# Packed attention with a gated convolution: gvl, the weights' sums, x, the last stores and the issue order changed together

## The chip, the cores and the metric

The kernel runs on one core of a Trainium2 chip. The metric is device time in microseconds, the median of several executions. In the texts PE is TensorE, DVE VectorE, ACT ScalarE, POOL GpSimd and SP SyncE, which issues all DMAs here.

## The reference

For 8 batches, 8 heads, 576 positions and a head size of 64, 32 packing queries p per head first attend to k and v; their 32 results are keys and values for the queries q. The 8 heads are put side by side (512 channels) as x. A causal convolution of 5 taps over x makes a gate, x @ w_val a value, and (gate * value) @ w_out is the output. q, k, v and p are float32, the three weights float64.

```python
p_packed = sm_attn(p, k, v)                  # 32 rows per head
out = sm_attn(q, p_packed, p_packed)         # 576 rows per head
x = out.transpose(0, 2, 1, 3).reshape(B, S, H * D)
gate_pre = sum(conv_w[k] * xp[:, k:k + S, :] for k in range(5))
gate = 1.0 / (1.0 + np.exp(-gate_pre))
val = x @ w_val
return gate * val @ w_out
```

## The kernel before

Each batch b goes through the same stages, written as generators: `load_k`, `load_v`, `load_q`, `load_p` (K, V, Q, P in the order), `keys` (k: p and k transposed on TensorE, kpt, kT), `attn_pack` (a: scores s1, softmax, at, pv, and ppd, the packed values twice side by side), `queries` (q: qpt, qT), `packed_turned` (p: ppT), `attn_out` (s: scores s2 of q with the packed keys, turned by VectorE into t, the maximum taken off by GpSimd, exp), `weighted` (t: t divided by its sum on GpSimd, turned back into a2, and split into a2h and a2l, the upper and lower parts in fp32r), `packed_values` (w: wp, packed values times w_val, split into wph and wpl), `mixed` (x), `gate` (g), `value` (v) and `project` (o). A head group g is 4 heads; an n4 or c of `gate`, `value` and `product` is one of 4 blocks of 128 channels. The trace calls s1 and s2 both s, told apart by what they read: s<-kT and s<-qT. In the same way a1 and a2 are called a there.

`mixed` (line 463) makes x, transposed, in PSUM, two halves of 288 positions per head group. For that the packed values pp, masked so that each head has its own columns, are split into pph and ppl, and six fp32r matmuls on tiles of 64 rows and 128 columns add pph·a2h, ppl·a2h and pph·a2l. ScalarE copies x to xp. `gate` (line 503) makes sig from xp: one step on ScalarE, four on VectorE (sig<-xp,cw,sig), and a tanh on ScalarE. `value` (line 523) multiplies sig by val on VectorE (gv), ScalarE rounds that to gvh, and GpSimd takes the difference, gvl; only the very last gvl is made on VectorE. `project` (line 576) has 36 chunks of 128 rows, 4 after an even batch and 5 after an odd one; each is 12 matmuls of 512 columns (gvh·woh, gvh·wol, gvl·woh for 4 blocks), a copy to osb, of which there are two buffers, and a store. The last batch holds its five chunks open in PSUM, and adds the last block to all of them at the end.

The weights come as 64-bit words. `from_double` (line 240) makes of each quarter a float32 upper part (top) and a lower part, in the words' own place: a scaling on ScalarE, and four steps on VectorE, or three and two more on ScalarE and GpSimd. `value_weights` (W, line 267) adds them on GpSimd to wv; `out_weights` (O, line 289) makes woh and wol.

The order of everything is written out in `ORDER` (line 49): each token lets a generator go one step (or so many), and so fixes the order of the instructions on each engine, SP's DMAs too. At the `|` the staging pool of the weights is closed and gvh and gvl are opened in its place. Every instruction is issued by the helper `InOrder`, so nearly all of them have line 94 in the profile.

Of the kernel before, what the change touches and what calls it, by code (L numbers as in the profile page):

```python
# [54 lines left out]
q1 t0 q1 g0 t0 w1 O0 g0 q1.2 w1 O0 q1.2 s1 O0 k2 q1 O0 s1 q1 K2 k2.2 V2 O0 s1 q1 Q2 k2.2 V2 k2 Q2 s1 K3 a2 P4 O0
s1.2 a2 s1 a2 k2 g0 k2.2 s1 g0 t0 v0 k2 g0 s1 t1 k2 s1 x0 v0 t1 k2 k3 | v0 a2 g0 x0 q2 k3 a2 v0 x0 q2 t1 q2 a2.3
x0 g0 v0 a2 q2 g0 x1 t1 x1 a2 q2 a2 t1 a2 q2.2 g0 a2.2 q2 t1 g0 x1 q2 g0 x1 v0 t1 a2 k3 q2 a2 x1 K3 x1 a2 V3 k3
g0 k3 Q3 v0 q2 P5 t1 k3.2 v0 q2 a2 t1 v0 k3 g0 a2 x1 t1 a2.3 g0 k3 a2.2 k3 g0 k3 a2.2 g0 p2 a3 g0 v0 p2 g0 k3.2
s2 v0 a3 k3 k4 v0 s2 a3 q3 s2 a3 q3 V3 g0 Q3 v0 K4 k4 a3 s2 K4 P6 a3.2 g0 a3 q3 s2 w2 g0 a3 q3 t2 g0 x1 a3 q3
a3.2 w2 v0 t2 a3.2 w2 v0 s2 q3 v0 g1 t2 o0 a3.2 t2 a3 g1 t2 s2 v1 o0 g1 s2 a3 g1 q3 a3.2 s2 x1 q3 o0 a3 Q4 o0 V4  # L60
x1 g1 s2 g1 t2 g1 v1 a3 t2 o0 k4 a3.2 o0 v1 g1 x1 k4 V4 t2 a3 v1 p3 x1 v1 a3 p3 t2 g1 x2 s3 t2 g1 q3 k4 s3 x2
q3.2 k4 o0 g1 q3 Q4 s3 g1 x2 g1 s3 v1.2 g1 q4 s3 k4 v1 q4.2 o0 K5 s3 k4 o0 q4 g1 k4 a4 s3 k4.2 g1 v1 k4 s3 g1 o0
a4 s3 g1.2 v1 a4 g1 s3 g1 v1 x2 o0 q4 g1 x2.2 o0 v1 q4 Q5 q4 x2 v1 q4 g1.2 x2.2 t3 g2 k4 v1 t3 x2 q4 K5 k4 k5 x2
v1 P7 g2 a4 q4 t3 x2 v1 o1 k5 a4 t3 x3 g2 a4.2 x3 t3 a4 o1 k5 t3 a4.2 o1 v2 k5 a4 g2 t3 a4 o1 a4 g2 t3 g2.2 v2
t3 q4 g2 v2 k5 Q5 t3 a4 q4 k5 g2 k5 o1 V5 w3 a4.2 v2 o1 k5 a4 K6 a4 k5 g2 a4.2 w3 o1 g2 k5 w3 a4 x3 g2.3 v2 o1
g2 o1 g2 o1 v2 g2 v2 g2 v2 g2 v2 o1 g2 o1 k5 g2 a4 x3 k5 v2 a4.2 g2 x3.2 v2 g2 V5 k5 a4 x3 a4 p4 v2 a5 K6 k5 p4
v2 g2 a5 x3 g3 a5 g3 o1 v2 g3 v2 g3 a5 v2 o1 v3 o1 a5 g3 a5 o2 a5 g3.2 v3 g3 v3 g3 a5 o2 k6 s4 v3 a5 o2 k6 x3 s4
q5 x3 a5 g3 x3 q5 a5 v3 s4 x3 g3 x4 s4 g3 a5 q5 g3 v3 o2 x4 s4 x4 g3 a5 q5 v3 t4 v3 a5 o2 s4 o2 a5.2 t4 V6 a5.2
q5 s4 a5.2 v3 q5 Q6 g3 a5 t4 g3 q5 t4 a5 s4 k6 q5 a5 w4 g3 k6 t4 g3 q5 k6 s4 g3 v3 a5 k6 w4 g3 x4 V6 o2 v3 g3 s4
# [590 lines left out]
```

## Time and profile before

| what | us |
|---|---|
| median of 3 runs | 331.21 (329.43 to 331.38) |
| profiled execution | 330.79 |
| its span, first to last instruction | 329.0 |
| PE / DVE / ACT / POOL busy in it | 287.6 / 259.0 / 215.3 / 123.2 |

The span is what the profile shows; some 1.8 us lie around it. Busy times overlap, and none of them is the time of the kernel. A group of rows names what an instruction writes and reads as out<-in, by the program's names without their numbers.

### The profile page before, as it was taken

The page shows a single profiled execution, that of the slowest core. Times are in us where ns is not written, and L with a number is a line of the kernel's source. Part 1 is how long each engine was busy: PE and PEld are TensorE (multiplying, and loading weights), DVE is VectorE, ACT ScalarE, POOL GpSimd, SP SyncE. Part 2 cuts the span into 40 slices and gives each one's busy share as a digit, 9 for nine tenths or more (in the row PEclk, how much of TensorE's full clock was granted, in tenths as well). Part 3 has the DMA queues.
Part 4 walks back from the last instruction along what each step waited for, and adds up shares of the span by engine and source line. Part 5 has one row for each costly group of instructions (what it writes and reads, how often), then busy time and mean ns, then how long its engine had stood idle before and what let it go on. Part 6 is the DMA issues. An engine that isn't in the chain of part 4 may idle for free.

```text
span 329.0 us, 7252 instructions
## 1 busy us (share of the span) xinstructions
PE 287.6 (87%) x2932; PEld 220.6 (67%) x2932; DVE 259.0 (79%) x381; ACT 215.3 (65%) x440; POOL 123.2 (37%) x115
## 2 busy tenths in 40 slices
PE   0157987979989999999999898989999999999990
PEld 0134744657758877877877677776868868778870
DVE  0794288689999999997797999998997899776600
ACT  0347788779986779777686867776677755655201
POOL 1334536374153455323245434415431237323200
PEclk9999997699999999999999999999999999999996
DMA  7999989495895765383507491635011011211013
GB/s 197 232 255 263 257 162 239 108 230 108 211 217 135 187 166 136 90 241 92 157 34 173 118 237 37 175 87 126 32 66 34 32 35 38 70 53 64 34 24 135
DMA packets 42474, 43.47 MB, mean 132 GB/s; under 512 B 6085, under 2 KB 36805, under 8 KB 42442
## 3 DMA queue, kind: packets, MB, share of 16 engines
q1 hardware_dynamic: 42442, 43.02, 53.6%
q8 instruction: 23, 0.38, 0.5%
q14 instruction: 9, 0.07, 0.1%
HBM read 33.57 MB, written 9.44 MB: 131 GB/s over the span
## 4 chain that ended last, share of the span: by engine, by line
PE 40%; DVE 31%; ACT 17%; issue 4%; DMA 3%; POOL 3%; SPq 1%; ACTq 0%; POOLq 0%
DVE sig L94 16%; PE o L94 15%; PE val L94 8%; ACT sig L94 4%; DVE a2l L94 3%; PE x L94 3%; PE s L94 3%; PE kpt L94 3%; PE pv L94 2%; DVE sm L94 2%; PE at L94 2%; DVE t L94 2%; DVE nb L94 2%; DMA wv_words<-in_moe_w_val_dram 2%; PE qpt L94 2%
## 5 line engine op out<-in xcount | busy, mean ns | idle before, releaser
L94 DVE SCALAR_TENSOR_TENSOR sig<-xp,cw,sig 128x576 f32<-128x576 f32 x128 | 122.6, 958 | 11.6 <-ACT sig L94 10.1
L94 POOL TENSOR_TENSOR gvl<-sig,gvh 128x576 fp32r<-128x576 f32 x31 | 49.1, 1584 | 80.0 <-ACT gvh L94 77.0
L94 PE MATMUL o<-woh,gvh 128*128 128x512 f32 x144 | 58.6, 407 | 0.8 <-ACT osb L94 0.8
L94 PE MATMUL o<-woh,gvl 128*128 128x512 f32 x144 | 56.5, 392 | 0.1
L94 PE MATMUL o<-wol,gvh 128*128 128x512 f32 x144 | 56.5, 392 | 0.0
L94 PE MATMUL val<-a2h,wph 128*128 128x288 f32 x128 | 39.6, 309 | 0.5 <-ACT a L94 0.5
L94 PE MATMUL val<-a2l,wph 128*128 128x288 f32 x128 | 37.9, 296 | 0.9 <-DVE a2l L94 0.9
L94 ACT COPY osb<-o 128x512 f32<-128x512 f32 x34 | 19.8, 582 | 28.3 <-PE o L94 22.6
L94 PE MATMUL val<-a2h,wpl 128*128 128x288 f32 x128 | 37.9, 296 | 0.0
L94 PEld LDWEIGHTS o<-woh,gvh 128*128 128x128 f32 x144 | 27.0, 188 | 10.3 <-issue 2.3
L94 ACT CAST gvh<-sig 128x576 fp32r<-128x576 f32 x32 | 21.7, 678 | 17.7 <-DVE sig L94 17.6
L94 POOL TENSOR_TENSOR t<-t,mx 128x576 f32<-128x576 f32 x16 | 24.2, 1513 | 22.0 <-DVE mx L94 22.0
L94 PEld LDWEIGHTS o<-woh,gvl 128*128 128x128 f32 x144 | 27.1, 188 | 6.6 <-POOL gvl L94 0.5
L94 ACT ACTIVATE sig<-sig 128x576 f32<-128x576 f32 x32 | 21.9, 686 | 13.1 <-DVE sig L94 12.9
L94 PEld LDWEIGHTS o<-wol,gvh 128*128 128x128 f32 x144 | 27.1, 188 | 4.6
L94 POOL TENSOR_TENSOR t<-t,rs 128x576 f32<-128x576 f32 x16 | 20.0, 1248 | 23.0 <-DVE rs L94 15.8
L94 DVE SCALAR_TENSOR_TENSOR sig<-sig,val 128x576 f32<-128x576 f32 x32 | 23.7, 741 | 5.6 <-PE val L94 3.0
L94 PE MATMUL qpt<-ident,qm 96*128 96x96 f32 x192 | 26.1, 270 | 1.1 <-ACT kT L94 1.1
L94 PE MATMUL kpt<-ident,km 96*128 96x96 f32 x192 | 26.8, 276 | 0.1
L94 PEld LDWEIGHTS val<-a2h,wph 128*128 128x128 f32 x128 | 24.2, 189 | 3.6 <-ACT a L94 1.2
L94 PEld LDWEIGHTS qpt<-ident,qm 96*128 96x128 f32 x192 | 21.0, 155 | 7.3 <-issue 4.3
L94 PEld LDWEIGHTS kpt<-ident,km 96*128 96x128 f32 x192 | 20.9, 156 | 6.9 <-issue 4.7
(87 smaller groups left out, 561.8 us busy)
## 6 DMA issues: line engine op xcount, KB each, us to landing
km<-in_k_dram SPq DMA_DIRECT2D x16, 576.0 KB, 7.4
vm<-in_v_dram SPq DMA_DIRECT2D x16, 576.0 KB, 6.1
qm<-in_q_dram SPq DMA_DIRECT2D x16, 576.0 KB, 6.0
out_dram<-osb SPq DMA_DIRECT2D x24, 256.0 KB, 2.2
wv_words<-in_moe_w_val_dram SPq DMA_DIRECT2D x8, 256.0 KB, 7.2
wo_words<-in_moe_w_out_dram SPq DMA_DIRECT2D x4, 512.0 KB, 10.0
out_dram<-osb SPq DMA_DIRECT2D x8, 192.0 KB, 2.3
p<-in_p_dram SPq DMA_DIRECT2D x16, 64.0 KB, 9.0
```

What stands on the lines that cost most here:

```text
L94: made = getattr(self.engine, op)(*args, **kw)
```

## The change

- gvl is made on VectorE for all batches and blocks.
- The upper and lower parts of w_val and w_out are added on TensorE: two float32 matmuls against the identity, into PSUM (`summed`). ScalarE copies the sum to wv, or halves it into woh; VectorE takes the difference wol out of PSUM. The branch of `from_double` that used GpSimd goes.
- x is made from a2 and ppd in float32: four matmuls of 288 columns per half, each on a tile of 32 rows and 64 columns. pp, the mask, pph and ppl go; ppd has two buffers.
- In the last batch the odd chunks are stored from t2's buffers and chunk 8 from a2's, so that the five chunks have five.
- `ORDER` is another one.

```diff
 ORDER = """
-K0 L0.3 V0 P0 W0.13 L0 W0 L0 W0 L0 Q0 W0 K0 W0 k0 P1 W0 k0.4 W0 k0.2 W0 C0 W0 k0 C0 a0 W0 C0 W0 a0 W0 a0 q0 C0
...
+x0 K0.2 P0 L0.2 Q0 L0.2 V0.2 k0 Q0 L0 k0.2 P1 k0.4 P2 W0 k0.2 W0 K1 k0.2 a0 W0 k0.2 W0 a0 k0 K1 W0.2 a0 W0 L0 a0
...
+    def summed(nm, words):
+        ps = one(f"{nm}_sum")
+        pe.matmul(ps, ident, st["top", nm], start=True, stop=False)
+        pe.matmul(ps, ident, words[:, :, 0].bitcast(F32), start=False, stop=True)
+        return ps
...
-            pool.tensor_tensor(
-                wv[:, c, :], st["top", f"wv{c}"], words[:, :, 0].bitcast(F32), op=ALU.add
-            )
+            ps = summed(f"wv{c}", words)
+            yield
+            act.copy(wv[:, c, :], ps)
...
-            yield from from_double(f"wo{c}", words, P, 0.5, True)
-            top, hi = st["top", f"wo{c}"], woh[:, c, :]
-            act.mul(top, top, 0.5)
-            yield
-            act.copy(hi, top)
-            yield
-            pool.tensor_tensor(top, top, hi.bitcast(F32), op=ALU.subtract)
-            yield
-            pool.tensor_tensor(wol[:, c, :], top, words[:, :, 0].bitcast(F32), op=ALU.add)
+            yield from from_double(f"wo{c}", words, P)
+            ps, hi = summed(f"wo{c}", words), woh[:, c, :]
+            yield
+            act.mul(hi, ps, 0.5)
+            yield
+            dve.scalar_tensor_tensor(
+                wol[:, c, :], ps, 0.5, hi.bitcast(F32), op0=ALU.mult, op1=ALU.subtract
+            )
...
-            dve.scalar_tensor_tensor(pp[:, g], pv2, rs, mask, op0=ALU.mult, op1=ALU.mult)
-            yield
...
-        act.copy(pph, pp)
-        yield
-        pool.tensor_tensor(ppl, pp, pph.bitcast(F32), op=ALU.subtract)
-        yield
...
-                for n, (w, x) in enumerate(((pph, ah), (ppl, ah), (pph, al))):
-                    for pr in range(2):
-                        pe.matmul(
-                            xps[:, pr, :HS],
-                            w[pairs[pr], g, :],
-                            x[pairs[pr], g, hc],
-                            start=(n == 0),
-                            stop=(n == 2),
-                        )
+                for hl in range(4):
+                    pe.matmul(
+                        xps[D * (hl % 2) : D * (hl % 2) + D, hl // 2, :HS],
+                        pp[heads[hl], g, 0, :],
+                        a2[heads[hl], g, hc],
+                        start=True,
+                        stop=True,
+                    )
...
-            (dve if b == B - 1 and n4 == NC - 1 else pool).tensor_tensor(
+            dve.tensor_tensor(
                 lo, gv, hi.bitcast(F32), op=ALU.subtract
             )
...
-            osb = tile_of("osb", [P, DM], F32, f"osb_{b}_{c}")
+            if b == B - 1 and c % 2:
+                osb = tile_of("t2", [P, G, NBLK, NP], F32, f"osb_{b}_{c}")
+                osb = osb.rearrange("a g y z -> a (g y z)")[:, :DM]
+            elif b == B - 1 and c == 8:
+                osb = tile_of("a2", [P, G, S], F32, f"osb_{b}_{c}")[:, 0, :DM]
+            else:
+                osb = tile_of("osb", [P, DM], F32, f"osb_{b}_{c}")
```

What the new order does on the engines is shown at two places. First ScalarE at the start, before; wv0 to wv3 are the four quarters of w_val, top their upper parts, words the loaded words, and the first digit of another name is the batch:

```order
L94 ACTIVATE wv0_top_100<-wv0_words_86 128x512
L94 ACTIVATE wv1_top_107<-wv1_words_89 128x512
L94 ACTIVATE wv2_top_114<-wv2_words_92 128x512
L94 ACTIVATE pT_0_138<-pTt_0_131 128x256
L94 COPY kT_0_0_140<-kpt_0_0_0_141 128x4x96
L94 ACTIVATE wv3_top_152<-wv3_words_116 128x512
```

ScalarE in the new kernel, from its third copy of a weight's sum to ppT of batch 0:

```order
L90 COPY wv_71<-wv2_sum_257 128x512
L90 ACTIVATE wv3_top_288<-wv3_words_98 128x512
L90 ACTIVATE ppd_0_226<-pv_0_0_263,sm1_0_0_183 128x128
L90 COPY a1t_0_1_294<-at_0_1_0_295 96x256
L90 COPY a1t_0_1_294<-at_0_1_1_302 96x256
L90 COPY a1t_0_1_294<-at_0_1_2_306 96x256
L90 ACTIVATE ppd_0_226<-pv_0_1_310,sm1_0_1_224 128x128
L90 ACTIVATE cw_top_343<-cw_words_110 5x512
L90 COPY wv_71<-wv3_sum_337 128x512
L90 COPY qT_0_1_349<-qpt_0_1_0_350 128x4x96
L90 ACTIVATE ppT_0_363<-ppTt_0_356 128x256
```

Three scalings stood at the head of ScalarE; now the scaling of each quarter stands behind the copy of the sum of the one before it, and ppT behind the last of these copies.

VectorE in the middle, around gv of batch 3 and block 1 (sig_3_1 with val_3_1), before:

```order
L94 SCALAR_TENSOR_TENSOR sig_3_1_2212<-xp_3_0_1976,cw_80,sig_3_1_2212 128x576
L94 SCALAR_TENSOR_TENSOR sig_3_1_2212<-sig_3_1_2212,val_3_1_2271 128x576
L94 SCALAR_TENSOR_TENSOR sig_3_2_2300<-xp_3_1_2137,cw_80,sig_3_2_2300 128x576
L94 TENSOR_REDUCE sm2_4_2324<-t2_4_2227 128x18
L94 TENSOR_TENSOR sm2_4_2324<-sm2_4_2324,eps_75 128x18
```

The same place in the new kernel:

```order
L90 SCALAR_TENSOR_TENSOR sig_3_1_2140<-sig_3_1_2140,val_3_1_2247 128x576
L90 SCALAR_TENSOR_TENSOR sig_3_2_2216<-xp_3_1_2005,cw_74,sig_3_2_2216 128x576
L90 TENSOR_REDUCE sm2_4_2295<-t2_4_2163 128x18
L90 TENSOR_TENSOR sm2_4_2295<-sm2_4_2295,eps_69 128x18
L90 RECIPROCAL rs2_4_2296<-sm2_4_2295 128x18
L90 TENSOR_TENSOR gvl_902<-sig_3_1_2140,gvh_901 128x576
```

gvl, which stood in GpSimd's queue, now stands four instructions behind its gv in VectorE's.

## Rows read from the trace of the kernel before

**Rows 1.** The page, its first part: busy us, share of the span, instructions.

```profile
PE 287.6 (87%) x2932; PEld 220.6 (67%) x2932; DVE 259.0 (79%) x381; ACT 215.3 (65%) x440; POOL 123.2 (37%) x115
```

**Rows 2.** Busy time of the engines by stretches; length, busy, PEclk, DMA share, GB/s.

```profile
0.00:40.00 40.00, 18.50 (x197) 13.96 (x198) 20.14 (x36) 18.71 (x41) 13.51 (x23) 1.00 1.04 241
...
40.00:100.00 60.00, 53.46 (x745) 35.81 (x744) 50.62 (x85) 50.93 (x113) 29.29 (x26) 0.91 0.87 182
...
180.00:290.00 110.00, 105.18 (x1026) 81.96 (x1025) 100.66 (x139) 76.22 (x149) 42.67 (x37) 1.00 0.32 85
...
100.00:321.00 221.00, 215.60 (x1994) 170.84 (x1992) 187.54 (x260) 144.53 (x286) 80.42 (x67) 1.00 0.37 99
```

**Rows 3.** Timeline of the start, all engines; start us, us, engine, instruction, [idle before].

```profile
8.97 0.66 ACT L94 ACTIVATE wv_top<-wv_words 128x512 f32<-128x512 f32 x1
...
10.86 0.43 DVE L94 TENSOR_SCALAR wv_words<-wv_top 128x512 uint32<-128x512 uint32 x1
...
11.32 0.69 DVE L94 SCALAR_TENSOR_TENSOR wv_words<-wv_words 128x512 f32<-128x512 uint32 x1
...
15.10 0.66 PE L94 MATMUL pTt<-ident,p 128*128 128x128 f32 x2 [15.10 <-DMA p<-in_p_dram]
...
22.69 1.28 POOL L94 TENSOR_TENSOR wv<-wv_top,wv_words 128x512 f32<-128x512 f32 x1 [2.77 <-DVE wv_words L94]
...
40.42 1.21 PE L94 MATMUL s<-qT,ppT 64*32 64x288 f32 x16
...
41.38 1.96 PE L94 MATMUL wp<-wv,ppT 64*32 64x512 f32 x16
```

**Rows 4.** Groups of instructions: busy us, mean ns | idle before and its end.

```profile
L94 DVE SCALAR_TENSOR_TENSOR sig<-xp,cw,sig 128x576 f32<-128x576 f32 x128 | 122.6, 958 | 11.6 <-ACT sig L94 10.1
...
L94 POOL TENSOR_TENSOR gvl<-sig,gvh 128x576 fp32r<-128x576 f32 x31 | 49.1, 1584 | 80.0 <-ACT gvh L94 77.0
...
L94 POOL TENSOR_TENSOR t<-t,mx 128x576 f32<-128x576 f32 x16 | 24.2, 1513 | 22.0 <-DVE mx L94 22.0
...
L94 POOL TENSOR_TENSOR t<-t,rs 128x576 f32<-128x576 f32 x16 | 20.0, 1248 | 23.0 <-DVE rs L94 15.8
...
L94 POOL TENSOR_TENSOR ppl<-pp,pph 128x256 fp32r<-128x256 f32 x8 | 7.1, 894 | 5.5 <-ACT pph L94 4.6 <-POOL gvl L94 0.9
...
L94 DVE SCALAR_TENSOR_TENSOR pp<-pv,sm,mask 128x128 f32<-128x128 f32 x16 | 5.4, 338 | 7.3 <-ACT ppd L94 7.2
...
L94 DVE TENSOR_TENSOR gvl<-sig,gvh 128x576 fp32r<-128x576 f32 x1 | 0.8, 759 | 0.7 <-ACT gvh L94 0.7
```

**Rows 5.** The tile sig: duration ns min/median/max, first and last start.

```profile
L94 DVE SCALAR_TENSOR_TENSOR sig<-xp,cw,sig x128: 718/818/2069, 58.7 to 307.1; 128x576 f32<-128x576 f32 x128
```

**Rows 6.** Timeline of VectorE and GpSimd near 204 us.

```profile
204.43 1.43 POOL L94 TENSOR_TENSOR gvl<-sig,gvh 128x576 fp32r<-128x576 f32 x1 [3.17 <-ACT gvh L94]
...
204.46 2.02 DVE L94 SCALAR_TENSOR_TENSOR sig<-xp,cw,sig 128x576 f32<-128x576 f32 x1
```

**Rows 7.** Timeline of the end: TensorE, ScalarE and SyncE's queue.

```profile
318.67 0.47 SPq L94 DMA_DIRECT2D out_dram<-osb  x1
...
319.87 0.54 SPq L94 DMA_DIRECT2D out_dram<-osb  x1
...
320.35 0.39 PE L94 MATMUL o<-woh,gvl 128*128 128x512 f32 x1
...
324.83 0.59 ACT L94 COPY osb<-o 128x512 f32<-128x512 f32 x1 [2.53 <-DMA out_dram<-osb]
...
325.44 0.35 SPq L94 DMA_DIRECT2D out_dram<-osb  x1
```

**Rows 8.** Timeline of TensorE in the middle: x, s and wp.

```profile
187.25 0.40 PE L94 MATMUL x<-a2h,pph 64*128 64x288 f32 x2
...
187.84 0.71 PE L94 MATMUL s<-qT,ppT 64*32 64x288 f32 x16
...
141.20 1.09 PE L94 MATMUL wp<-wv,ppT 64*32 64x512 f32 x16
```

More of the change, by code (lines that the diff above doesn't have):

```diff
@@ L28 @@
  'pT': 1,
- 'pp': 2,
- 'ppd': 1,
+ 'ppd': 2,
  'ppT': 2,
- 'pph': 1,
- 'ppl': 1,
  'qT': 2,
@@ L55 @@
[L55 to L69, printed above, removed]
@@ L83 @@
+g6 v6 o5 g6 o5 g6 x7 a7 o5 g6 v6 a7 g6 v6.2 g6 a7 o5 g6 o5 v6 a7 g6.2 p7 o5 g6 v6 p7 g6 v6 g6 v6 s7 o5 g6 v6 o5
+s7 g6 o5 s7 g6 s7 v6.2 s7 v6 s7 o5 w7 t7 o5 o6 s7 t7 w7 s7 t7 s7 w7 t7 x7 o6 t7 s7 o6.2 x7 t7.2 x7 o6 t7 o6.2 t7
+x7.2 t7 g7.2 v7 o6 g7 o6 g7 x7 g7 o6 g7.2 v7 x7 g7 v7 g7 x7 o6 v7.2 o6 x7 g7.2 o7 g7.2 v7 g7 v7 g7 v7.2 g7 o7
+g7.3 v7 g7 v7.3 o7 g7.4 o7 v7.3 o7.15
 """
@@ L177, in packed_attention_gated_conv @@
     heads = [slice(NP * hl, NP * hl + NP) for hl in range(4)]
-    pairs = [slice(2 * NP * pr, 2 * NP * pr + 2 * NP) for pr in range(2)]
-    mask = const.tile([P, 2, D], F32, name="mask")
-    nc.gpsimd.memset(mask, 0.0)
-    for hl in range(4):
-        nc.gpsimd.memset(mask[heads[hl], hl % 2, :], 1.0)
     eps = const.tile([P, G * NBLK], F32, name="eps")
@@ L238, in load_weights, with from_double @@
             yield
-    def from_double(nm, words, rows, by=1.0, rest_on_pool=False):
+    def from_double(nm, words, rows):
         top = st["top", nm] = tile_of("top", [P, DM], F32, f"{nm}_top", stage)[:rows]
@@ L258, in from_double @@
         yield
-        if rest_on_pool:
-            pool.tensor_tensor(rest, rest, hw.bitcast(F32), op=ALU.mult)
-        else:
-            dve.scalar_tensor_tensor(
-                rest, lw, 2.0**-52 * by, hw.bitcast(F32), op0=ALU.mult, op1=ALU.mult
-            )
-        yield
+        dve.scalar_tensor_tensor(
+            rest, lw, 2.0**-52, hw.bitcast(F32), op0=ALU.mult, op1=ALU.mult
+        )
+        yield
+    def summed(nm, words):
[3 more added lines that the diff above has]
+        return ps
     def value_weights(b):
@@ L463, in mixed @@
     def mixed(b):
-        pp = st["pp", b].rearrange("a g x d -> a g (x d)")
-        pph = tile_of("pph", [P, G, P], F32R, f"pph_{b}")
-        ppl = tile_of("ppl", [P, G, P], F32R, f"ppl_{b}")
-        act.copy(pph, pp)
-        yield
-        pool.tensor_tensor(ppl, pp, pph.bitcast(F32), op=ALU.subtract)
-        yield
         for g in range(G):
@@ L477, in mixed @@
                 hc = slice(half * HS, half * HS + HS)
[L478 removed]
+                pp, a2 = st["ppd", b], st["a2", b]
                 xps = big(f"x_{b}_{g}_{half}")
[L480 to L488 removed]
+                for hl in range(4):
[5 more added lines that the diff above has]
+                        stop=True,
+                    )
                 yield
```

52 lines of the change are left out of this document (29 added, 23 removed).

## Prediction

> **What bounds the kernel now.** I read the page first, then the busy time by stretches, then the groups of instructions, and last three short timelines: the start, one piece of the middle, the end. The page gives TensorE (PE) the most busy time of all engines, 287.6 us of a span of 329.0 [rows 1]. The stretches tell where the rest is lost. From 100 to 321 us TensorE is busy for 215.6 of 221 us, 97.6%, and VectorE (DVE) for 187.5, 85% [rows 2]: the middle belongs to TensorE, with VectorE close behind in 180 to 290, where it reaches 100.7 of 110 us. In the first 100 us TensorE is busy for 18.5 of 40 and 53.5 of 60 us [rows 2], so it loses 28 us there, against 5.4 us in all of the middle. The first timeline says why: nothing runs on TensorE until 15.10 us, when p lands behind the weights, and the first scores of the second attention (s<-qT) start at 40.42 [rows 3]. The end is a third place: the last matmul starts at 320.35 and lasts 0.39, but the last store is copied only at 324.83 and issued at 325.44 [rows 7]. So three places can give time: the start, the 5.4 us of the middle, and some 3 us of the end.
>
> The sum is made against the profiled execution: 330.8 us, a span of 329.0 and 1.8 around it, 0.4 below the median of 331.2.
>
> **The end: five store buffers.** The last five chunks go out through two osb buffers now. ScalarE's last copy, at 324.83, is held back by a store's landing: 2.53 us idle before it, ended by the DMA [rows 7]. With a buffer for each chunk, the copies wait for TensorE alone: 320.35 + 0.39 + 0.59 (one copy) is 321.3. SyncE then sets the pace: seven issues in a row, of which the first starts at 318.67 and the third at 319.87 [rows 7], 0.60 us apart. The seventh starts at 318.67 + 6 x 0.60 = 322.3 instead of 325.44. That is -3.1 us. The transfers themselves get closer together; if they then share their way, the gain shrinks towards 2, and if issues take only 0.47, it is 3.9.
>
> **gvl on VectorE, pp and its halves gone.** GpSimd (POOL) makes 31 gvl tiles for 49.1 us, and ppl for 7.1; both leave it. VectorE makes the last gvl already, in 759 ns, so it gains 31 x 0.76 = 23.6 us, and loses the 16 pp for 5.4 [rows 4]. It also loses waiting: its 128 gate steps (sig<-xp) have a mean of 958 ns and a median of 818 [rows 4, 5]; above the median that makes 128 x 0.14 = 17.9 us. A step that started beside a gvl shows it: 2.02 us at 204.46, with GpSimd's gvl from 204.43 [rows 6]. GpSimd keeps its two t operations, 24.2 + 20.0 us [rows 4]; of its four large groups 56.2 of 100.4 us leave, 56%, so I take 10.0 us of the 17.9 back. VectorE nets 23.6 - 5.4 - 10.0 = +8.2 us; if no wait goes it is +18.2, if all go +0.3. Spread over the 240 us from 70 to 310 that is 3%, on an engine at 85% (91% in 180 to 290), beside TensorE at 97.6%. TensorE hides it, and the new order puts each gvl a step or two behind its gv, so that ScalarE's rounding in between (gvh) is done. What is late next is then TensorE itself. The cover is thin where VectorE is busiest, so the bounds for the middle are -5.4 (all of TensorE's idle time goes) and +8 (VectorE binds in the 110 us from 180 to 290, where 110/240 of 18.2 is 8.3 us of work, and each of them lengthens the stretch). I take -1.0, near to nothing, since TensorE has only 5.4 to give.
>
> **x from a2 in float32.** A half of x is six matmuls on 64x128 tiles now, and costs 187.84 - 187.25 = 0.59 us until the next instruction [rows 8]. In its place come four on 32x64 tiles. No row shows such a tile. The nearest is s: eight float32 matmuls of the same 288 columns, on 64x32 tiles, side by side, for 0.71 us with its end [rows 8]; without it, as the 0.59 is counted, a little less. I take 0.62; 28 of the 32 halves lie where TensorE binds: 28 x 0.03 = +0.9 us. If all go as fast as the six, it is 0. The other bound is a rival, below. x now also needs nothing but a2 and ppd, so a2l and the halves of pp are off its path; but a2 has one buffer, and the next batch's transposition must wait for x. The order has about 18 us of VectorE work between the two, by the row times, and I cost it at nothing.
>
> **The start.** Both halves of k and p are loaded first. Two transfers of 0.59 MB (96x4x384 floats) at 241 GB/s [rows 2] are 4.9 us, so p lands at about 8 and TensorE starts there, 7 us earlier. Against it stands the new way of the weights. Today ScalarE's scalings run ahead, and the last sum is made by GpSimd at 22.69 + 1.28 = 24.0 [rows 3]. In the new order each quarter's scaling stands on ScalarE behind the copy of the quarter before, which waits for TensorE's sum, which waits for VectorE: a chain. A quarter is 0.66 + 0.43 + 0.69 + 0.43 + 0.69 = 2.9 us (one scaling and four steps on VectorE) [rows 3], a copy of 0.6, and a sum of two float32 matmuls of 512 columns. Nothing like it is in the trace; wp streams 512 columns in two rounds on tiles side by side, for 1.09 us in the middle and 1.96 at 41 us [rows 3, 8], so two of them are 2.2 to 3.9. A quarter is 5.7 to 7.4 us, four are 23 to 30, and from about 12 us the chain ends at 35 to 42. ppT stands behind that on ScalarE, and the first s<-qT behind ppT: 37 to 45, against 40.42. I take 39, because TensorE is busier there than today, and -2.0 us for the start, with bounds of -8 (the whole lead of 7 us and a little of the idle time) and +5. TensorE's eight sums, 18 to 31 us, lie in stretches where it idles for 28.
>
> The output weights take the same chain four times, behind the first batch's x; their cover is the gate of batch 0. Loads move too: q's second half and both of v now come before the output weights. That is inside the bounds of the start.
>
> **Sum:** 330.8 - 3.1 - 1.0 + 0.9 - 2.0 = 325.6 us.
>
> **Rivals.** First, no change worth the name: the start loses what it wins. For it speaks the chain through four engines, against it TensorE's idle 28 us. With +3 instead of -2 at the start and nothing from the middle the time is 330.8 - 3.1 + 0.9 + 3 = 331.6; between 328 and 334.
>
> Second, slower: the four tiles of x don't run side by side. Two of them lie in different rows of the array and write the same PSUM bank, in different partitions; in s each half of the rows has a bank of its own. From s to wp, 224 more columns cost 1.09 - 0.71 = 0.38 us [rows 8], so 288 columns cost 0.49. As two pairs, one after the other, a half of x costs 0.49 more, and 28 halves 13.7: 325.6 + 13.7 = 339.3. It decides from 0.1 us a half on. For it speaks only that no row has this layout; against it that s keeps eight tiles going at once.
> The Trainium skill's page "TensorEngine Tiling (Array Packing)", under "Restrictions and Gotchas", says that different row tiles write to different PSUM banks and can't access the same bank at the same time. By that rule this rival holds; no run here has shown two row tiles in one bank.
>
> Third, slower as well: VectorE binds. For it speaks its share in 180 to 290, against it the 56% of GpSimd's work that goes. If no wait goes, VectorE gains 18.2 us of work and the middle 8: 330.8 - 3.1 + 8 + 0.9 - 2 = 334.6.
>
> Fourth, faster than forecast: the lead at the start holds (-8) and the middle gives 4: 330.8 - 3.1 - 4 + 0.9 - 8 = 316.6.
>
> **How the numbers follow.** Forecast (321 to 328): 0.38. Faster (313 to 321): 0.15. No change: 0.25. x one pair after another: 0.11. VectorE: 0.11. A measurement of this kernel tells about 1% from no change, 3.3 us. Faster by more than that, below 327.9: nearly all of the first two, 0.52. Within it: 0.26. Slower, above 334.5: 0.22. The range, 315 to 338, leaves out the quick end of the fourth rival and the second rival's 339: the tail of both, 2 in 10. The likeliest case's own range is 321 to 328.
>
> **What would show it.** At the end, the last issue under 2.5 us after TensorE's last matmul, and no copy idle for a DMA. On VectorE, a mean of sig<-xp near 880 ns, and gvl at 0.76. In x, eight records within 0.7 us: over 1 us means the second rival. The first s<-qT at 37 to 41 and TensorE at or above 97% from 100 us on. I am wrong in the step of the start if s<-qT comes after 43; in the middle if VectorE is at 97% and TensorE falls below 95%; and altogether if the sum of these steps is right and the time is not.

## The result and the profile after

| what | before | after |
|---|---|---|
| median, us | 330.44 (329.43 to 331.38) | 318.89 (317.48 to 320.38) |
| profiled execution, us | 330.79 | 318.79 |
| its span, us | 329.0 | 316.7 |

The new kernel takes 0.965 of the time (95% interval 0.960 to 0.971): 11.5 us less, where 5.2 were forecast. The time lies in the forecast's range of 315 to 338 and on its side, but below its likeliest case (321 to 328), where the fourth rival stood (313 to 321, price 316.6). All ratios are of executions in the faster of two states, and only the fifteenth experiment has one in the slower state, which its median contains.

The page's first part, of the kernel after:

```profile
PE 292.0 (92%) x3028; PEld 210.3 (66%) x3028; DVE 256.5 (81%) x404; ACT 211.1 (67%) x428; POOL 44.8 (14%) x55
```

Against [rows 1] TensorE does 4.4 us more, VectorE 2.5 less, and GpSimd 78.4 less. The stretches, with the columns of [rows 2] (start:end, length, busy us of PE, PEld, DVE, ACT and POOL with their instructions, PEclk, which is the clock granted to TensorE as a share of full speed, DMA share, GB/s):

```profile
0.00:40.00 40.00, 27.37 (x299) 15.10 (x299) 17.47 (x35) 20.07 (x45) 1.96 (x9) 1.00 1.06 221
40.00:100.00 60.00, 53.79 (x648) 34.94 (x645) 56.69 (x96) 46.05 (x100) 11.40 (x12) 1.00 1.01 203
...
20.00:30.00 10.00, 7.65 (x115) 3.73 (x115) 4.90 (x12) 4.69 (x13) 0.00 (x0) 1.00 1.18 228
...
50.00:90.00 40.00, 35.08 (x445) 23.18 (x445) 38.51 (x64) 31.91 (x71) 6.66 (x7) 1.00 1.08 207
...
100.00:310.00 210.00, 209.82 (x2085) 159.71 (x2085) 181.67 (x273) 144.04 (x284) 31.43 (x34) 1.00 0.39 101
```

The last three of these stretches are not among [rows 2]. The last of them read, in the kernel before:

```profile
100.00:310.00 210.00, 204.86 (x1948) 162.27 (x1947) 186.09 (x258) 143.80 (x285) 80.42 (x67) 1.00 0.38 103
```

From 100 to 310 us TensorE is now hardly ever idle (busy for 209.82 of 210 us, before 204.86). In the first 40 us it works 27.4 us instead of 18.5. And there is a stretch in which VectorE is the busier one: from 50 to 90 us it is busy for 38.51 of 40 us and TensorE for 35.08, where before it was 33.94 and 36.09.

The timeline of the start, of the kernel after: when p, k, the first scaling, the first sum, VectorE's last step for it, the last scaling, the last copy, s<-qT and x come.

```profile
9.20 0.66 PE L90 MATMUL pTt<-ident,p 128*128 128x128 f32 x2 [9.20 <-DMA p<-in_p_dram]
9.65 3.41 PE L90 MATMUL kpt<-ident,km 96*128 96x96 f32 x20
...
11.55 0.67 ACT L90 ACTIVATE wv_top<-wv_words 128x512 f32<-128x512 f32 x1
...
14.68 1.05 PE L90 MATMUL wv_sum<-wv_top,ident 128*128 128x512 f32 x2
...
14.98 0.69 DVE L90 SCALAR_TENSOR_TENSOR wv_words<-wv_words 128x512 f32<-128x512 uint32 x1
...
15.73 1.17 PE L90 MATMUL wv_sum<-wv_words,ident 128*128 128x512 f32 x2
...
27.67 0.68 ACT L90 ACTIVATE wv_top<-wv_words 128x512 f32<-128x512 f32 x1
...
32.11 0.58 ACT L90 COPY wv<-wv_sum 128x512 f32<-128x512 f32 x1 [1.15 <-PE wv_sum L90]
...
33.61 1.18 PE L90 MATMUL s<-qT,ppT 64*32 64x288 f32 x16
...
42.35 0.71 PE L90 MATMUL x<-a,ppd 32*64 32x288 f32 x8 [0.56 <-DVE a L90]
42.99 0.55 PE L90 MATMUL qpt<-ident,qm 96*128 96x96 f32 x4
```

The two groups on VectorE that answer to [rows 4]:

```profile
L90 DVE SCALAR_TENSOR_TENSOR sig<-xp,cw,sig 128x576 f32<-128x576 f32 x128 | 107.5, 840 | 5.9 <-ACT sig L90 4.8
...
L90 DVE TENSOR_TENSOR gvl<-sig,gvh 128x576 fp32r<-128x576 f32 x32 | 24.6, 769 | 2.5 <-ACT gvh L90 2.3
```

gvl on VectorE costs the 0.77 us that the forecast took, and a gate step 840 ns on the mean instead of 958. The end, which answers to [rows 7]; ScalarE's copies wait for TensorE alone:

```profile
308.97 3.90 SPq L90 DMA_DIRECT2D out_dram<-osb  x7
...
310.67 0.39 PE L90 MATMUL o<-woh,gvl 128*128 128x512 f32 x1
311.10 0.58 ACT L90 COPY osb<-o 128x512 f32<-128x512 f32 x1 [0.77 <-PE o L90]
```

Where the 12.3 us of the spans went is read from three marks: the first o, the last matmul and the end. The first o stands at 98.76 before, and after at:

```profile
91.07 0.40 PE L90 MATMUL o<-woh,gvh 128*128 128x512 f32 x1
```

| stretch | before | after | difference | forecast |
|---|---|---|---|---|
| start to the first o | 98.76 | 91.07 | -7.7 | -2.0 |
| first o to the last matmul | 221.6 | 219.6 | -2.0 | -0.1 (middle -1.0, x +0.9) |
| last matmul to the end of the span | 8.65 | 6.03 | -2.6 | -3.1 |

So the start carries most of what the forecast lacks.

### The profile page after: what moved, and what is told of

It reads as the page before. It is cut to its first block, busy times and chain, and to the rows that moved or that the text cites. A ratio compares the mean times of both kernels' runs of the same rounds, so it can differ in the third digit from the quotient of the medians.

```text
span 316.7 us, 7391 instructions
## 1 busy us (share of the span) xinstructions
PE 292.0 (92%) x3028; PEld 210.3 (66%) x3028; DVE 256.5 (81%) x404; ACT 211.1 (67%) x428; POOL 44.8 (14%) x55
## 4 chain that ended last, share of the span: by engine, by line
PE 69%; DVE 15%; ACT 6%; DMA 5%; issue 1%; SPq 0%; POOL 0%; POOLq 0%; DVEq 0%; ACTq 0%
PE o L90 26%; PE val L90 13%; DVE sig L90 6%; PE s L90 5%; PE x L90 5%; PE kpt L90 4%; PE qpt L90 4%; PE pv L90 3%; DMA qm<-in_q_dram 3%; PE at L90 3%; PE wv_sum L90 2%; PE wp L90 2%; DMA p<-in_p_dram 2%; DVE sm L90 2%; ACT sig L90 2%; DVE wo_words L90 1%
## 5 line engine op out<-in xcount | busy, mean ns | idle before, releaser
L90 DVE SCALAR_TENSOR_TENSOR sig<-xp,cw,sig 128x576 f32<-128x576 f32 x128 | 107.5, 840 | 5.9 <-ACT sig L90 4.8
L90 POOL TENSOR_TENSOR t<-t,mx 128x576 f32<-128x576 f32 x16 | 22.9, 1432 | 110.3 <-DVE mx L90 110.3
L90 PEld LDWEIGHTS kpt<-ident,km 96*128 96x128 f32 x192 | 20.2, 151 | 11.9 <-issue 4.8
L90 ACT COPY qT<-qpt 128x384 f32<-128x384 f32 x48 | 23.2, 486 | 6.8 <-PE qpt L90 6.5
L90 PE MATMUL kpt<-ident,km 96*128 96x96 f32 x192 | 25.7, 266 | 2.0 <-DVE wol L90 1.0
L90 DVE TENSOR_TENSOR gvl<-sig,gvh 128x576 fp32r<-128x576 f32 x32 | 24.6, 769 | 2.5 <-ACT gvh L90 2.3
L90 ACT COPY kT<-kpt 128x384 f32<-128x384 f32 x48 | 22.9, 483 | 4.2 <-PE kpt L90 4.0
```

The costliest lines, as they stand in the source:

```text
L90: made = getattr(self.engine, op)(*args, **kw)
```

## The experiments

"Loss" and "gain" are against the kernel that was edited, 318.9 for the new one and the median of the kernel before in the same series for the old one. The new kernel was not run again in these series, and the medians of the kernel before in them lie between 329.74 and 330.64. Where the interval of a ratio overlaps the new kernel's, 0.960 to 0.971, a difference from it is not shown; that is so for the ninth, the tenth and the fourteenth to eighteenth, and by a little for the fourth. Three theories were in play for the start. Theory L: the loads and the order behind them give it. Theory W: the sums on TensorE give it. The chain: the weights' quarters, one after the other, set its end. For the middle the question was whether gvl on VectorE gives more than the 1 us that was forecast.

**1. The new kernel with the loads in the old order.**

```diff
-x0 K0.2 P0 L0.2 Q0 L0.2 V0.2 k0 Q0 L0 ...
+x0 K0 L0.3 V0 P0 L0 Q0 K0 V0 k0 Q0 L0 ...
```

> The changed kernel with the loads of the start in the order of before (k's first half, three quarters of w_val, v's first half, p, the last quarter, q, and only then k's second half); all else as changed. Theory L, the unforeseen 6 us of the start come from k and p landing first: 4 to 6 us lost, 323 to 325, TensorE's first instruction at 14 to 16 us. Theory W, they come from the weights' new way and the order of the engines, not from the loads: at most 1.5 us lost, under 320.5.

Measured: 331.90 us, 1.006 of before (1.004 to 1.008), a loss of 13.0, more than the whole gain. The timeline of TensorE at the start:

```profile
23.06 1.51 PE L90 MATMUL kpt<-ident,km 96*128 96x96 f32 x8 [4.92 <-DMA km<-in_k_dram]
...
26.34 1.50 PE L90 MATMUL wv_sum<-wv_top,ident 128*128 128x512 f32 x2
...
46.50 0.72 PE L90 MATMUL s<-qT,ppT 64*32 64x288 f32 x16
```

p is turned at 15.56, as theory L had it, but the loss is twice the 4 to 6 us that it allowed, and theory W falls. The new order puts k's second half ahead of the first sum on TensorE. Loaded late, it holds the whole chain of the weights: the first sum starts 11.7 us later, s<-qT 12.9, the first o 12.5 (103.53). What is late at s<-qT is here about as late at the end.

**2. The eight sums back on GpSimd.**

```diff
-            ps = summed(f"wv{c}", words)
+            pool.tensor_tensor(
+                wv[:, c, :], st["top", f"wv{c}"], words[:, :, 0].bitcast(F32), op=ALU.add
+            )
...
-            ps, hi = summed(f"wo{c}", words), woh[:, c, :]
-            yield
+            ps, hi = st["top", f"wo{c}"], woh[:, c, :]
+            pool.tensor_tensor(ps, ps, words[:, :, 0].bitcast(F32), op=ALU.add)
+            if c < NC - 1:
+                yield
             act.mul(hi, ps, 0.5)
-            yield
+            if c < NC - 1:
+                yield
...
```

> The changed kernel with the eight sums of the weights' parts back on GpSimd, at the same places of the order. Theory L: TensorE has idle time there, so no difference beyond 1.5 us, 317.5 to 320.5. Theory W, TensorE's sums keep GpSimd out of VectorE's way and TensorE at its higher rate from 16 us on: 3 to 6 us lost, 322 to 325, with s of 1.2 us again at 30 us.

Measured: 323.18 us, 0.980 of before (0.975 to 0.985), a loss of 4.3, in theory W's range of 3 to 6. Its sign, an s of 1.2 us near 30 us, says nothing, as the new kernel's s at 33.61 takes 1.18. TensorE is relieved of sixteen matmuls of 512 columns, and the kernel got slower. Its first s<-qT comes earlier, at 31.19, but the first o later, at 95.08. One stretch shows why one must not read the early s<-qT as a gain:

```profile
20.00:30.00 10.00, 5.53 (x110) 4.76 (x110) 6.07 (x11) 4.10 (x11) 3.52 (x3) 0.50 1.17 226
```

From 20 to 30 us TensorE is busy for 5.53 of 10 us, at a granted clock of 0.50, the lower of its two levels (1.2 of 2.4 GHz); the new kernel has 7.65 and 1.00 there. Whether the clock or GpSimd cost the time was left to the eleventh and thirteenth. The edit does one thing more than move the sums, and so do theirs: for the last quarter of w_out there is no `yield` (a step of the order) between the sum, woh and wol, so that wol stands earlier in VectorE's queue, ahead of a, where in the new kernel it stands behind it.

**3. gvl back on GpSimd, all but the last.**

```diff
-            dve.tensor_tensor(
+            (dve if b == B - 1 and n4 == NC - 1 else pool).tensor_tensor(
                 lo, gv, hi.bitcast(F32), op=ALU.subtract
             )
```

> The changed kernel with gvl back on GpSimd except for the last. Theory M, VectorE is hidden behind TensorE: 0 to 3 us lost, 319 to 322. Theory V, VectorE's relief from GpSimd is worth more than the work it takes over: over 5 us lost, 324 or more, gate steps back at a mean of 940 ns or more.

Measured: 325.27 us, 0.985 of before (0.981 to 0.989), a loss of 6.4, on theory V's side (over 5, a mean of 940 ns or more). The first o stands at 91.38, that of the new kernel at 91.07, and from there to the last matmul it takes 224.4 us instead of 219.6, so the middle carries it (in the profiled execution, 323.55 us, it is 4.8 us in all). Its groups:

```profile
L90 DVE SCALAR_TENSOR_TENSOR sig<-xp,cw,sig 128x576 f32<-128x576 f32 x128 | 127.5, 996 | 8.7 <-ACT sig L90 7.0
...
L90 POOL TENSOR_TENSOR gvl<-sig,gvh 128x576 fp32r<-128x576 f32 x31 | 50.1, 1615 | 86.0 <-ACT gvh L90 85.8
```

128 gate steps cost 996 ns each instead of 840, 20.0 us in all. VectorE saves 31 gvl of 0.77 us, 23.8 us, and is as busy as in the new kernel nevertheless (182.72 against 181.67 us from 100 to 310 us), while TensorE has 2.8 us of idle time there again:

```profile
100.00:310.00 210.00, 207.17 (x2069) 156.17 (x2068) 182.72 (x248) 143.19 (x282) 74.70 (x62) 1.00 0.39 101
```

The Trainium skill's page "SBUF — State Buffer", under "Who interferes with whom", says that a VectorE instruction with two inputs in SBUF contends with a GpSimd instruction that reads SBUF. These steps read two tensors, and their mean falls and rises with GpSimd's gvl (996 ns with it, 840 without; in the old order 958 and 854, experiment 6); the trace agrees.

**4. The last batch through two store buffers again.**

```diff
-            if b == B - 1 and c % 2:
-                osb = tile_of("t2", ...
...
+            osb = tile_of("osb", [P, DM], F32, f"osb_{b}_{c}")
```

> The changed kernel with the last five chunks through two osb buffers again. From the prediction's step: 3.1 us lost (2 to 3.9), 321 to 322.8; from the two profiles, where the end after TensorE's last matmul is 5.8 us instead of 8.3: 2.5 us lost. If the transfers share their way, so that the buffers change nothing: under 1 us.

Measured: 321.73 us, 0.974 of before (0.969 to 0.978), a loss of 2.8, near the 3.1 of the prediction. The last copies wait for landings as in [rows 7]:

```profile
312.48 0.58 ACT L90 COPY osb<-o 128x512 f32<-128x512 f32 x1 [3.10 <-DMA out_dram<-osb]
```

**5. The kernel before with k's second half and p loaded first.**

```diff
-K0 L0.3 V0 P0 W0.13 L0 W0 L0 W0 L0 Q0 W0 K0 W0 k0 ...
+K0.2 P0 L0.3 V0 W0.13 L0 W0 L0 W0 L0 Q0 W0 W0 k0 ...
```

> The kernel before with one edit: the second half of k and p are loaded ahead of the first three quarters of w_val, as in the new kernel; the order on the engines stays. Theory L (early loads give the lead by themselves): TensorE's first matmul near 9 us, the first s<-qT 4 to 7 us earlier than 40.42, the time 323 to 327 us. Rival I (loads and engine order only work together): pT stands on ScalarE behind the scalings of three quarters, which now land some 5 us later, and VectorE's steps on w_val start later too; the first s<-qT at 40 to 46 and the time 329 to 335 us.

Measured: 334.52 us, 1.010 of before (1.007 to 1.013), a loss of 3.9, rival I. TensorE starts at 8.76, and then waits 7.29 us for pT, which stands on ScalarE behind three scalings of weights. The first of them now starts at 12.46 instead of 8.97, and the third waits 2.92 us for GpSimd's sum:

```profile
8.76 0.66 PE L94 MATMUL pTt<-ident,p 128*128 128x128 f32 x2 [8.76 <-DMA p<-in_p_dram]
...
17.99 0.90 PE L94 MATMUL kpt<-ident,km 96*128 96x96 f32 x4 [7.29 <-ACT pT L94]
...
43.89 1.21 PE L94 MATMUL s<-qT,ppT 64*32 64x288 f32 x16
```

So the loads by themselves lose, and without them the new order loses: each needs the other.

**6. The kernel before with gvl on VectorE**, the edit of the third the other way round.

> The kernel before with gvl on VectorE at the places where the old order has it. Theory V (GpSimd's gvl cost VectorE more than it saved): the mean of sig<-xp falls from 958 to 830 to 880 ns and the time to 324 to 328 us. Rival (gvl on VectorE needs the new order): gvl now waits there for ScalarE's rounding, which stands right before it, up to 0.7 us for each of 31, so that what contention gives back is lost in waits; the mean of sig<-xp falls as much, but the time is 329 to 338 us.

Measured: 329.08 us, 0.995 of before (0.993 to 0.998), a gain of 1.6. Neither theory has it whole. Contention goes (854 ns for a gate step instead of 958), but gvl waits hardly at all for its rounding, 1.2 us in all, so the rival's mechanism falls:

```profile
L94 DVE SCALAR_TENSOR_TENSOR sig<-xp,cw,sig 128x576 f32<-128x576 f32 x128 | 109.3, 854 | 7.8 <-ACT sig L94 6.4
...
L94 DVE TENSOR_TENSOR gvl<-sig,gvh 128x576 fp32r<-128x576 f32 x32 | 23.5, 735 | 1.2 <-ACT gvh L94 1.1
```

VectorE's sum of both is 132.8 us, against 123.4 before, so it has 9 us more to do in these two groups. TensorE gains 1.6 us of busy time from 100 to 310 us (206.46 of 210, before 204.86), which is of the size of the gain.

**7. The kernel before with the eight sums on TensorE**, at the old places.

```diff
-            pool.tensor_tensor(
-                wv[:, c, :], st["top", f"wv{c}"], words[:, :, 0].bitcast(F32), op=ALU.add
-            )
+            ps = summed(f"wv{c}", words)
+            act.copy(wv[:, c, :], ps)
...
```

> The kernel before with the eight sums of the weights on TensorE and the copies on ScalarE, at the places of the old order. Theory W (the sums themselves help: TensorE has work while it idles, GpSimd is out of VectorE's way): 324 to 328 us, the undoing of the second experiment. Rival (they help only where p's and k's work is early too): within 2 us of 329.7, because TensorE has nothing before 15 us and the copies lie on ScalarE's path.

Measured: 348.27 us, 1.052 of before (1.048 to 1.055), a loss of 17.6. Both theories fall. In the old order the sums stand ahead of p on TensorE, and wait there for VectorE and, at 17.37, for 2.43 us for the second quarter to land:

```profile
11.30 2.04 PE L94 MATMUL wv_sum<-wv_top,ident 128*128 128x512 f32 x2 [11.30 <-DVE wv_top L94]
...
20.43 0.63 PE L94 MATMUL pTt<-ident,p 128*128 128x128 f32 x2
...
49.87 0.72 PE L94 MATMUL s<-qT,ppT 64*32 64x288 f32 x16
```

p is turned at 20.43 instead of 15.10, s<-qT starts at 49.87 instead of 40.42, and the first o at 115.04 instead of 98.76. Where the further 7 us between these two marks come from was not taken apart.

**8. The kernel before with gvl on VectorE, the sums on TensorE and five store buffers.**

> The kernel before with three parts of the change (gvl on VectorE, the sums on TensorE, five store buffers), in the old order and with the old x. Theory P (the parts of the code carry the gain): 318 to 322 us. Rival O (the order, its loads among it, carries the start's 8 us and keeps VectorE from waiting for the roundings): 325 to 334 us, of which the five buffers alone give 3.

Measured: 344.02 us, 1.040 of before (1.036 to 1.043), a loss of 13.4. The same three parts, put into the new order with the new x, belong to a kernel that is 11.5 us faster. This was further than rival O went, and near the sum of the parts (17.6 - 1.6 - 2.8 = 13.2, the last from the fourth experiment): without the order they lose, by the sums.

**9. The new kernel with p loaded ahead of k.**

```diff
-x0 K0.2 P0 L0.2 Q0 ...
+x0 P0 K0.2 L0.2 Q0 ...
```

> The new kernel with p loaded ahead of both halves of k. TensorE's first matmul waits for p until 9.20 us there, and from there to 34 us it idles only some 3 us. Theory T (from its first matmul on, TensorE sets the time, so each us of an earlier start counts): pT at 3 to 4 us, the first half of k turned from about 6 us on, 1 to 2 us less in the end, 316.5 to 318 us. Rival W (the weights' quarters set the time of the first s<-qT): 318.2 to 319.5 us.

Measured: 320.77 us, 0.971 of before (0.968 to 0.974), 1.9 above the new kernel. TensorE starts at 3.50 and is then idle three times, for 2.40, 0.43 and 1.93 us; the first sum's first pair, which took 1.05 us, takes:

```profile
14.47 1.96 PE L90 MATMUL wv_sum<-wv_top,ident 128*128 128x512 f32 x2
```

After the earlier start with gaps TensorE has its slower rate for longer, and s<-qT comes at 34.69 instead of 33.61. Both theories miss that.

**10. As the ninth, and each quarter of w_val scaled ahead of the copy of the sum before it.**

```diff
             ps = summed(f"wv{c}", words)
+            if c < NC - 1:
+                scaled(f"wv{c + 1}", st["words", "wv"][c + 1], P)
             yield
             act.copy(wv[:, c, :], ps)
```

> As the ninth, and ScalarE scales the next quarter of w_val ahead of the copy of a sum, not behind it, which cuts the chain of the quarters. In the new kernel TensorE idles 0.96 and 2.08 us before the second and third sum, for VectorE's steps behind these scalings. Theory C (the chain costs what TensorE waits there): 2 to 3 us less than the ninth, 314 to 316 us. Rival T (what TensorE does not wait there it waits a little later, for the same order's other edges): within 1 us of the ninth.

Measured: 319.63 us, 0.968 of before (0.964 to 0.971), 1.1 less than the ninth in the same series. s<-qT comes 3.3 us earlier, at 31.39, and a third of that reaches the end: near the rival's "within 1 us".

**11. The new kernel with the four sums of w_out on GpSimd**, those of w_val left on TensorE; the second part of the second experiment's diff.

> The new kernel with the four sums of w_out on GpSimd, those of w_val left on TensorE. Eight matmuls of 1.1 us go from TensorE in a stretch where it is busy for 54 of 60 us. Theory T (TensorE's own work sets the time there): 311 to 316 us. Rival G (the sum on GpSimd is slower, holds VectorE, and wol behind it is what TensorE waits for; so the second experiment's 4.3 us come mostly from w_out): 320 to 324 us. If the 4.3 us came from w_val alone: 317.5 to 319.5 us.

Measured: 325.70 us, 0.987 of before (0.982 to 0.992), a loss of 6.8, on rival G's side and beyond its 320 to 324. What TensorE waits for most between 12 and 92 us, in total, times and longest:

```profile
PE x L90 <- DVE a L90: 6.1, 3, 2.8
```

And the stretch from 50 to 90 us:

```profile
50.00:90.00 40.00, 30.91 (x328) 22.14 (x323) 33.10 (x55) 26.31 (x56) 10.68 (x9) 0.67 0.68 145
```

TensorE's clock is down to 0.67, and VectorE is no longer full. (The profiled execution took 328.34 us, the longest of the four.)

**12. The new kernel without 36 products.**

```diff
         for n, (w, x) in enumerate(((gvh, woh), (gvh, wol), (gvl, woh))):
+            if n4 == 0 and n == 1:
+                continue
```

> The new kernel without the products gvh x wol of the first block of channels: 36 matmuls of 512 columns are left out. Theory T (from 100 us on nothing but TensorE's work sets the time): 36 x 0.39 = 14.1 us less, 304 to 306 us. Rival V (VectorE, 87% busy there, or the chain through the gate is close behind): 3 to 9 us less, 310 to 316 us.

Measured: 314.26 us, 0.951 of before (0.948 to 0.954), 4.6 less than the new kernel, in rival V's range. The 0.39 us of the expectation was the wrong number: such matmuls overlap, and start 0.23 us apart, so that 36 of them are 8.2 us. Of these 56% come out at the end. Of the other 3.6 us, 1.7 are idle time of TensorE, which was 0.12 us from 100 to 300 and is now 1.8; the rest was not traced:

```profile
100.00:300.00 200.00, 198.22 (x2030) 149.26 (x2029) 178.85 (x270) 141.75 (x280) 31.54 (x36) 1.00 0.41 105
```

So TensorE's work sets most of the time from 100 us on, and something stands close behind it; VectorE, busy for 178.85 of 200 us, is the likeliest, which is argued and not shown.

**13. As the eleventh, with the eight matmuls left on TensorE.** They read wv and write to a place that nothing reads; the sums are GpSimd's.

```diff
+            unread = one(f"wo{c}_unread")
+            for n in range(2):
+                pe.matmul(unread, ident, wv[:, n, :], start=(n == 0), stop=(n == 1))
```

> As the eleventh (the four sums of w_out on GpSimd), but at each of their places TensorE still gets the two matmuls of 512 columns, now from wv, into a place that nothing reads; they wait for nothing. The eleventh lost 6.8 us to the new kernel, its TensorE waited three times 2.8 us for a, and its granted clock fell to 0.50 to 0.94 from 40 to 90 us. Theory C (TensorE's own work kept its clock, and with the work gone the same matmuls take twice as long): the clock stays at 1.00 and the time is 318.5 to 320.5 us. Rival G (GpSimd's sums delay VectorE and a, and TensorE waits for that): the waits of 2.8 us stay, 324 to 327 us.

Measured: 325.77 us, 0.989 of before (0.984 to 0.994), the eleventh's time. Its stretch from 50 to 90 us, and what TensorE waits for most:

```profile
50.00:90.00 40.00, 31.64 (x351) 21.84 (x349) 34.34 (x56) 26.98 (x58) 10.53 (x9) 0.87 0.84 169
```

```profile
PE x L90 <- DVE a L90: 5.3, 3, 2.8
```

With the work kept, the clock is up from 0.67 to 0.87, waits of up to 2.8 us for a are still there, and the median is the same. So the eight matmuls cost nothing where they are put back. More does not follow, for two reasons.

Theory C's condition, a clock of 1.00, was not met. At 52.56 us, the third half of x, TensorE is even with the new kernel (52.78). At the next s<-qT, 61.19, it is 3.0 us late (58.21): it has waited 1.24 us for the turned a, and from 58.0 to 61.3 its granted clock is 0.50, so that twelve val matmuls take 3.23 us instead of 1.82, of which one is

```profile
58.42 0.44 PE L90 MATMUL val<-a2h,wpl 128*128 128x288 f32 x1
```

And the longest wait hangs on the place of wol. The chain of waits before it, by start, us and what, runs from the sum of the last quarter on GpSimd through woh and wol into VectorE's queue, where a stands, to x:

```profile
74.08 1.29 POOL wo_top L90
...
75.39 0.64 ACT woh L90
...
76.05 0.69 DVE wol L90
...
77.47 0.70 DVE a L90
...
78.31 0.76 PE x L90 x8
```

VectorE is idle for 2.11 us before this wol, which by the edit stands ahead of a. In the new kernel a comes first, at 70.69, and wol at 74.07, where nobody waits for it. How much of the 6.8 us is GpSimd's slower sum by itself, how much the moved wol and how much the clock stays open.

**14. The new kernel with 40 matmuls of the identity ahead of p.**

```diff
+    unread = one("unread")
+    for n in range(40):
+        pe.matmul(unread[:, :P], ident, ident, start=True, stop=True)
```

> The new kernel with 40 matmuls of the identity by itself (128 columns, into a place that nothing reads) at the head of TensorE's queue, while it waits for p until 9.20 us. There the same 288-column s takes 1.21 us at 12.99 and 0.72 at 16.82. Theory R (the slow rate at the start costs what the durations say): kpt, s and the first sum take half as long from the start, the first s<-qT at 31 to 33 instead of 33.61, 316 to 318 us. Rival A (ScalarE's copies and the weights' chain set the pace there): 318.2 to 319.5 us.

Measured: 320.58 us, 0.970 of before (0.968 to 0.973), 1.7 above the new kernel. The added matmuls were too many and held p back by 2.9 us, to 12.10:

```profile
1.42 10.85 PE L90 MATMUL unread<-ident 128*128 128x128 f32 x80 [1.42 <-POOL ident masks.py:199]
...
12.32 1.99 PE L90 MATMUL kpt<-ident,km 96*128 96x96 f32 x20
```

But kpt takes 1.99 us where it took 3.41, and s<-qT is only 1.5 us late, at 35.14. Theory R has the rate right, but neither its s<-qT (31 to 33) nor its end.

**15. The new kernel with the quarters scaled ahead**, the edit of the tenth without that of the ninth.

> The new kernel with the next quarter of w_val scaled ahead of the copy of a sum, and the loads as they are. In the tenth this brought the first s<-qT from 34.69 to 31.39 us and the end only 1.0 us forward, because TensorE then waited for k's next halves. Theory T (TensorE's own work and k's loads set the time, the chain of the quarters hardly): 317.5 to 319.5 us. Rival C (the chain): 315 to 317 us.

Measured: 316.79 us, 0.958 of before (0.954 to 0.961), in rival C's range of 315 to 317. But the ratio's interval overlaps the new kernel's, so that a small gain is likely and not shown.

**16 and 17. The fifteenth with 40 and with 26 matmuls of the identity ahead of p.**

> The fourteenth and the fifteenth together, a candidate for a faster kernel. If both gains hold and add up: 314 to 316.5 us. If the start is set by the loads of k: within 1 us of the better of the two.

> As the sixteenth with 26 instead of 40 matmuls of the identity. In the fourteenth the 40 took 10.85 us from 1.42 on, so that p's first matmul came 2.9 us late, at 12.10; kpt then took 1.99 us where it took 3.41, and the first s<-qT was only 1.5 us late. 26 of them, 0.27 us each, end near 8.5 us. If the quick rate gives these 1.4 us and they reach the end: 314 to 316 us, below the fifteenth's 316.8. If kT's copies, the loads of k or the places where TensorE waits later take them back: 316 to 318.5 us.

Measured: 318.71 us, 0.965 of before (0.962 to 0.969), outside both ranges, and 317.34, 0.960 (0.957 to 0.963), in the second one's. With 26 p is not held back much, kpt takes 1.99 us from 9.92 on, and the first x comes at 40.52 instead of 42.35; the end does not follow.

**18. The fifteenth with the quarters of w_out scaled ahead too.**

> As the fifteenth, and the quarters of w_out are scaled ahead as well. In the new kernel TensorE waits 1.4 us for wo_words and 1.4 us for wol between 47 and 65 us. If these waits are on the path: 314 to 316 us. If VectorE's queue, through which a and the gate of batch 0 go as well, sets the pace there: within 1 us of the fifteenth's 316.8.

Measured: 318.41 us, 0.962 of before (0.960 to 0.965), so nothing more, and outside both ranges. Its trace shows where a lead goes:

```profile
30.40 0.94 PE L90 MATMUL s<-qT,ppT 64*32 64x288 f32 x16
...
73.85 0.44 PE L90 MATMUL val<-a2h,wpl 128*128 128x288 f32 x1
...
91.06 0.40 PE L90 MATMUL o<-woh,gvh 128*128 128x512 f32 x1
```

```profile
70.00:80.00 10.00, 8.69 (x78) 6.98 (x63) 8.79 (x16) 7.43 (x17) 2.76 (x2) 0.83 0.83 153
```

s<-qT is 3.2 us ahead of the new kernel's, the first o only 0.01. At the first x 2.1 us are left (40.26 against 42.35), at the first val 1.6 (54.88, 56.45): TensorE has waited for k and v to land, up to 1.1 us at a time. At the second group of twelve val there are still 1.5 (73.50, 74.98). These val take 0.44 us each where the new kernel's take

```profile
75.20 0.29 PE L90 MATMUL val<-a2h,wpl 128*128 128x288 f32 x1
```

for the granted clock is 0.83 from 70 to 80 us, where it was 1.00; at the next x the lead is gone (77.37, 77.30). VectorE is not full there: it is busy for 36.70 us from 50 to 90, and waits 1.9 us for val. So in this trace the loads and TensorE's lowered clock end the lead, not VectorE's work. In the seventeenth the clock stays at 1.00 from 50 to 90 us, and of a lead of 2.4 us at s<-qT 0.4 reach the first o (90.65).

No version with the full work beats the new kernel by more than the intervals leave open. One that the numbers suggest, w_val's sums on GpSimd and w_out's on TensorE (the second lost 2.5 us less than the eleventh), wasn't tried.

## Why the prediction was right and wrong

**The start: -2.0 forecast, -7.7 measured, and this is the step that failed.** The forecast put "four are 23 to 30, and from about 12 us the chain ends at 35 to 42" and took s<-qT at 39. The chain began at 11.55 and its last copy ended at 32.69: the scalings stand at 11.55, 17.41, 22.88 and 27.67, so a quarter is 5.3 us on the mean, below the low end of 5.7. Two things make the chain that short. A sum's first matmul needs only the upper part, and runs while VectorE still makes the lower one (14.68, against VectorE's last step of that quarter from 14.98 on). And its two pairs took 1.05 and 1.17 us, the quick end of what was allowed. s<-qT came at 33.61, 5.4 us ahead of the 39: 2.0 of these are the choice of 39 over the low end of 37, 2.3 the chain's end (32.69 instead of 35), and 1.1 the way from there to s<-qT (0.9 instead of 2). The lead of 6.8 us over the kernel before stayed whole up to the first o (57.5 us from s<-qT to it, 58.3 before). The bound of -8 held it. "TensorE starts there, 7 us earlier" was near: 9.20 against 15.10, 5.9 us.

The forecast priced the early loads and the chain as two terms of one sum. The first and fifth experiments show that they are one edit: the loads without the order lose 3.9 us, the order without the loads 13.0. Nor does the chain set the start alone: with s<-qT 3.2 us earlier (experiment 18), the first o did not move, as the lead went into waits for loads and a stretch at the lower clock.

**The middle: -1.0 forecast, and without x some -3 measured.** From the first o to the last matmul it is -2.0, in which x's cost is contained (below). The marks do not part the same work, as 8 halves of x now lie ahead of the first o and 6 did before, so this is no closer than an us. The mis-sized term is "I take 10.0 us of the 17.9 back". The 128 gate steps fell from 122.6 to 107.5 us, 15.1 back; their mean is 840 ns, not "near 880". VectorE's net is 23.8 - 5.4 - 15.1 = +3.3 us instead of +8.2. A term that the forecast left out comes to it: a2l, which reads two tensors as well, fell from 1055 to 750 ns, 4.9 us in all. TensorE's idle time in 100 to 310 fell from 5.1 us to 0.2, so nearly all of the 5.4 that the forecast saw there was taken. That TensorE hides the rest held. In the new order gvl on VectorE is worth 6.4 us (experiment 3), in the old one 1.6 (experiment 6).

**x: +0.9 forecast.** Eight records in 0.71 us, and 42.99 - 42.35 = 0.64 us until the next instruction, against 0.59 before and 0.62 taken: 28 x 0.05 = +1.4. The second rival falls, as one pair after the other would have cost 0.49 us more. Two row tiles write one PSUM bank in different partitions, and all run side by side. The new x by itself in the kernel before wasn't tried. The page "TensorEngine Tiling (Array Packing)" of the Trainium skill says, under "Restrictions and Gotchas", that row tiles can't use the same bank at once; here the measurement differs from it and decides.

**The end: -3.1 forecast, -2.6 measured in the spans, 2.8 by experiment 4.** No copy waits for a landing, and of the seven issues, which run from 308.97 for 3.90 us, the last starts at 312.47, so that they are 0.58 us apart, where 0.60 was taken.

**The rivals.** No change and VectorE as the bound fell with the time. The fourth came out, at its own prices nearly: -8 and -4 stood for -7.7 and some -3. It had 0.15, because the start was taken at 39, above the low end of a chain whose links were added up whole. The forecast's sign, s<-qT at 37 to 41, was the first to fail.

## What to carry to other kernels

Price a new order by the queue in which a late operand stands, not part by part: here two edits that lose 3.9 and 17.6 us alone belong to a kernel that gains 11.5. When a chain through several engines is added up, let each link start with what it needs first, not when the whole of the link before is done. And before shortening a chain further, follow a lead through the trace to the end: one of 3 us at 30 us was gone at 77, into waits for loads and a lowered clock. Where an edit moves work to another engine, also compare the queues of the others: a step that changed its place with it (wol) held VectorE for 2.1 us in the thirteenth.
